# Loads and value products of the attention in another order, ahead of a fused expert network

## The chip, the cores and the metric

The kernel runs on one core of a Trainium2 chip. The metric is the device time of one launch in microseconds, as the median of several runs. One execution is also taken by the hardware profiler, and all rows below come from it.

## The reference

There are 12,480 tokens of 128 features (q, k, v, all float32) and 49 agents of 128 features. Three stages follow one another:

- Agent attention. The agents look at all keys: softmax over the 12,480 keys of scale * agents @ k.T, times v, gives 49 x 128 agent values. Every token then looks at the agents: softmax over 49 of scale * q @ agents.T, times the agent values. scale is 1 / sqrt(128).
- First expert layer: h = x @ w_in (128 to 2048), g = h where h > 0, else exp(h) - 1, then g @ w_out (2048 to 128).
- Second expert layer: h = y @ w_in2, g = max(h, 0) + alpha * min(h, 0) with one alpha per hidden feature, then g @ w_out2.

The result is 12,480 x 128 float32.

## The kernel before

**Three stretches.** A prologue computes the agents' attention over all keys. `normalize` turns its sums into agent values, and `fold` multiplies these with the first weight matrix, so that the main loop can go from a token's 49 shares straight to the first hidden layer. The main loop takes 25 blocks of 384 to 512 tokens and, in each, 8 units of 256 hidden features through four products: g1 (shares by folded weights), g2 (back to 128 features), g3 (second layer up), g4 (down). g3 and g4 run 10 units behind g1 and g2. Most products are split into a high and a low part, three matmuls for one.

**The prologue in pieces.** Keys and values are cut into ten pieces of 1280 tokens (the last of 960). For piece i, `scores` (S) makes 10 products with the agents (L478), copies them from PSUM with ACT (L488) and takes a running maximum with DVE (L491). Pieces 0 to 4 are one half, 5 to 9 the other. `max_down` (D) and `max_across` (X) turn a half's maximum into a row that every partition has (L500, L501, L502, L506). `weigh` (E) subtracts it with DVE (L511), exponentiates with ACT (L515) and sums on POOL (L518); the last piece of a half has DVE reduce the sum (L520). `values` (A) multiplies the weights with v's piece into one PSUM bank (L549); the fifth of each half copies the half's result out (L558). `shares` (N) makes the reciprocal of the sum (L529 to L540). Q are steps of the first token block's own softmax.

**The words.** The weights lie in memory as 64-bit words and are decoded on the chip. There are 16 slices, w0 to w15: w0 to w3 the first matrix, w4 to w7 the second, then wi2 (w8, w9, w10, w12) and wo2 (w11, w13, w14, w15). `decode` has three steps: two ACT instructions that read the words (L337, L338; this frees the word buffer), then DVE's two bit steps (L346, L349) and POOL's sum (L360, or L355 for w0 to w3), then ACT's high part and the low part (L366, L367), the latter on DVE for w8 and w9 and on POOL for the others. `micro(2)`, written T2 in the order, takes two such steps, from at most two slices in flight. What is left of the words when the prologue ends is decoded in the first slots of the main loop, two steps at each of four places of a slot from the second slot on; wo2 only after all four folds.

**What sets the order.** `LOADS` is the order in which SP issues the loads. `pump` goes down this list as far as buffers are free: k and v share a ring of nine, words have a ring of four. A k buffer is freed by its S, a v buffer by its A, and a word buffer by the first decode step. `ORDER` is the order in which the prologue's parts are written. S, D, X, E, A and N are written with a priority of 20. Only SP keeps the written order in the prologue (`PINNED`); the queues of PE, ACT, DVE and POOL are ordered at build time by a planner that looks at priorities, the written order and its own times for each instruction.

**PSUM.** The pairs of banks that S writes come from a ring of three, and a decode step of the prologue uses the same ring for its scratch (`spare`).

Of the kernel before, what the change touches and what calls it, by code (L numbers as in the profile page):

```python
# [36 lines left out]
SLICES += [("wi2", 0), ("wi2", 1), ("wi2", 2), ("wo2", 0), ("wi2", 3), ("wo2", 1), ("wo2", 2), ("wo2", 3)]  # L37
WO1, WI2, WO2 = [[SLICES.index((n, j)) for j in range(4)] for n in ("wo1", "wi2", "wo2")]
LOADS = """
    w0 k0 w1 k1 q0 w2 k2 w3 k3 w4 k4 k5 w5 k6 k7 k8 k9 w6 v0 v1 w7 v2 v3 v4 w8 v5 v6 w9 v7 v8 w10 v9 a0 q1  # L40
    w11 w12 w13 w14 w15
"""
ORDER = """
    T2 S0 T2 S1 Q2 T2 S2 Q2 S3 T2 Q2 S4 D0 Q2 T2 S5 X0 E0 Q2 S6 T2 E1 Q2 S7 E2 T2 S8 Q2 E3 T2 Q2 S9 D1 E4 A0 X1 A1 T2
    E5 A2 E6 T2 Q1 A3 E7 A4 E8 T2 A5 E9 N0 T2 A6 T2 A7 T2 A8 T2 A9
"""
PRIORITY = 20
REST_DVE = (8, 9)
# [771 lines left out]
```

## Time and profile before

| | |
|---|---|
| median of 3 runs | 1092.75 us (1092.57 to 1095.7) |
| profiled execution | 1091.42 us |
| its span, first to last instruction | 1089.3 us |
| PE busy | 1056.3 us (97%), mean granted clock 0.985 |
| DVE busy | 833.5 us (77%) |
| ACT busy | 818.2 us (75%) |
| POOL busy | 627.6 us (58%) |
| moved by DMA | 41.34 MB, mean 38 GB/s |

The slices of the page cut the span in 40 equal parts of 27.2 us; a digit is the busy share in tenths. A load of k or v is 640 KB (the last piece 480 KB), one of words 512 KB, of q for one block up to 256 KB. The score products and the value products appear as two PE instructions each, so a whole piece has 20.

### The profile page before, as it was taken

To read this page: it belongs to the slowest core of one execution; us is meant where nothing else is said; L and a number is where in the kernel's file an instruction comes from. 1 tells how busy PE (TensorE), PEld (TensorE's weight loads), DVE (VectorE), ACT (ScalarE), POOL (GpSimd) and SP (SyncE) were. 2 spreads that over 40 slices of the span, in tenths; PEclk is the share of its full clock that TensorE was granted. 3 is DMA by queue.
4 is the path that set the end of the run, shared out by engine and by line. 5 is a ranking of instruction groups with operands and counts; after the bars stand their busy time and mean duration, and the time that the engine had idled before them with its cause. 6 is when DMAs were issued, how large, how long until landed. Compare 5 with 4: busy or idle time off the path is not lost.

```text
span 1089.3 us, 13465 instructions
## 1 busy us (share of the span) xinstructions
PE 1056.3 (97%) x5045; PEld 839.5 (77%) x5045; DVE 833.5 (77%) x930; ACT 818.2 (75%) x954; POOL 627.6 (58%) x357
## 2 busy tenths in 40 slices
PE   7776999999999999999999999999999999999998
PEld 7744888888888877777777777777777777777776
DVE  5875588787878878878878788788788787888653
ACT  5687677778777787778777777877877777777763
POOL 3768555555655656556655665565565565565440
PEclk9878999999999999999999999999999999999999
DMA  9920000100100000010010010010010000000000
GB/s 359 371 86 19 10 18 19 28 10 20 29 19 19 20 20 19 20 29 11 21 29 11 21 29 10 20 30 10 20 30 13 27 20 18 23 10 20 10 1 20
DMA packets 17915, 41.34 MB, mean 38 GB/s; under 512 B 3345, under 2 KB 6303, under 8 KB 17851
## 3 DMA queue, kind: packets, MB, share of 16 engines
q1 hardware_dynamic: 17707, 40.36, 11.4%
q8 instruction: 40, 0.66, 0.3%
q14 instruction: 24, 0.20, 0.1%
q10 hardware_dynamic: 144, 0.13, 0.0%
HBM read 27.60 MB, written 6.39 MB: 31 GB/s over the span
## 4 chain that ended last, share of the span: by engine, by line
PE 90%; DVE 3%; POOL 2%; ACT 2%; issue 1%; DMA 1%; SPq 0%; POOLq 0%; DVEq 0%; ACTq 0%
PE o L418 10%; PE o L420 9%; PE o L419 9%; PE h L419 8%; PE h L420 8%; PE h L418 8%; PE h L617 8%; PE y L418 8%; PE y L419 8%; PE y L420 8%; PE h L620 4%; PE h L478 1%; POOL gl L646 1%; PE h L158 0%; PE h L157 0%
## 5 line engine op out<-in xcount | busy, mean ns | idle before, releaser
L646 POOL TENSOR_TENSOR gl<-g,gh 128x1024 fp32r<-128x1024 f32 (+2 forms) x200 | 468.4, 2347 | 264.4 <-DVE gh L637 169.9
L679 DVE SCALAR_TENSOR_TENSOR xl<-h,xh 128x1024 fp32r<-128x1024 f32 (+3 forms) x201 | 239.7, 1193 | 126.1 <-ACT xh L678 124.5
L678 ACT ACTIVATE xh<-h 128x1024 fp32r<-128x1024 f32 (+3 forms) x201 | 201.3, 1002 | 178.2 <-PE h L420 176.9
L635 DVE SCALAR_TENSOR_TENSOR g<-e,h 128x1024 f32<-128x1024 f32 (+2 forms) x200 | 236.5, 1183 | 80.7 <-ACT e L628 58.3
L627 ACT ACTIVATE e<-h 128x1024 f32<-128x1024 f32 (+2 forms) x200 | 199.3, 997 | 28.6 <-PE h L620 27.8
L628 ACT ACTIVATE e<-e 128x1024 f32<-128x1024 f32 (+2 forms) x200 | 208.1, 1040 | 6.1
L418 PE MATMUL o<-xh,wo2h 128*128 128x512 f32 (+2 forms) x400 | 161.8, 405 | 0.0
L419 PE MATMUL y<-gl,wo1h 128*128 128x512 f32 (+2 forms) x400 | 155.7, 389 | 2.4 <-POOL gl L646 2.4
L418 PE MATMUL h<-yh,wi2h 128*128 128x512 f32 (+2 forms) x400 | 154.3, 386 | 3.1 <-ACT yh L664 3.1
L418 PE MATMUL y<-gh,wo1h 128*128 128x512 f32 (+2 forms) x400 | 156.0, 390 | 0.0
L420 PE MATMUL y<-gh,wo1l 128*128 128x512 f32 (+2 forms) x400 | 154.9, 387 | 0.0
L420 PE MATMUL h<-yh,wi2l 128*128 128x512 f32 (+2 forms) x400 | 154.5, 386 | 0.0
L419 PE MATMUL h<-yl,wi2h 128*128 128x512 f32 (+2 forms) x400 | 154.5, 386 | 0.0
L420 PE MATMUL o<-xh,wo2l 128*128 128x512 f32 (+2 forms) x400 | 154.1, 385 | 0.0
L419 PE MATMUL o<-xl,wo2h 128*128 128x512 f32 (+2 forms) x400 | 153.8, 384 | 0.0
L617 PE MATMUL h<-pst,s 128*128 128x512 f32 (+2 forms) x400 | 110.1, 395 | 3.9 <-POOL gl L646 1.6
L637 DVE SCALAR_TENSOR_TENSOR gh<-e,h 128x1024 fp32r<-128x1024 f32 (+1 forms) x94 | 112.7, 1199 | 0.0
L644 ACT CAST gh<-g 128x1024 fp32r<-128x1024 f32 (+2 forms) x106 | 107.4, 1013 | 3.2 <-DVE g L635 3.1
L418 PEld LDWEIGHTS o<-xh,wo2h 128*128 128x128 f32 x400 | 74.9, 187 | 29.0 <-ACT xh L678 11.8
L617 PEld LDWEIGHTS h<-pst,s 128*128 128x128 f32 x400 | 75.5, 191 | 21.9 <-issue 2.6
L419 PEld LDWEIGHTS y<-gl,wo1h 128*128 128x128 f32 x400 | 76.0, 190 | 18.5 <-POOL gl L646 4.0
L418 PEld LDWEIGHTS h<-yh,wi2h 128*128 128x128 f32 x400 | 75.2, 188 | 17.8 <-ACT yh L664 3.4
(143 smaller groups left out, 1297.6 us busy)
## 6 DMA issues: line engine op xcount, KB each, us to landing
vt<-in_vm_dram SPq DMA_DIRECT2D x9, 640.0 KB
kt<-in_kT_dram SPq DMA_DIRECT2D x8, 640.0 KB
q<-in_qT_dram SPq DMA_DIRECT2D x18, 256.0 KB
psq<-pst SPq DMA_DIRECT2D x72, 64.0 KB
out_dram<-o SPq DMA_DIRECT2D x17, 256.0 KB
wi<-in_w_in_dram SPq DMA_DIRECT2D x8, 512.0 KB
wo<-in_w_out_dram SPq DMA_DIRECT2D x8, 512.0 KB
q<-in_qT_dram SPq DMA_DIRECT2D x6, 240.0 KB
```

The lines of the kernel that those rows point to most:

```text
L418: nc.tensor.matmul(out, w_hi, x_hi, start=start, stop=False)
L419: nc.tensor.matmul(out, w_hi, x_lo, start=False, stop=False)
L420: nc.tensor.matmul(out, w_lo, x_hi, start=False, stop=stop)
L617: nc.tensor.matmul(h_t[u + v][:, c, :], s1[:, i + 2 * v + c, :], pst[b][:, :n], start=True, stop=False)
L627: nc.scalar.activation(out=e, in_=h_t[u], func=AF.Relu, scale=-1.0)
L628: nc.scalar.activation(out=e, in_=e, func=AF.Exp, scale=-1.0)
L635: nc.vector.scalar_tensor_tensor(out=g, in0=e, scalar=-1.0, in1=h, op0=ALU.add, op1=ALU.max)
L637: nc.vector.scalar_tensor_tensor(out=gh, in0=e, scalar=-1.0, in1=h, op0=ALU.add, op1=ALU.max)
L644: nc.scalar.copy(out=gh, in_=g)
L646: nc.gpsimd.tensor_tensor(out=gl, in0=g, in1=gh.bitcast(F32), op=ALU.subtract)
L678: nc.scalar.activation(out=xh[:, c, :], in_=h[:, c, :], func=AF.Relu)
L679: nc.vector.scalar_tensor_tensor(out=xl[:, c, :], in0=h[:, c, :], scalar=0.0, in1=xh[:, c, :].bitcast(F32), op0=ALU.max, op1=ALU.subtract)
```

## The change

Two strings are changed and nothing else. In the loads, k2 comes ahead of w2, k4 ahead of w3, and so on; v0 to v9 start after k6 and lie between the last k; w5, w6 and w7 come between the later v, and w8, w9 and w10 after v9 and q1. In the order, A0 stands behind E1, A1 behind E2, A2 behind E3, A3 behind E4 and A4 behind X1, where all five stood behind E4 or later. Some T2 stand elsewhere, and there are thirteen of them instead of fifteen.

```diff
 LOADS = """
-    w0 k0 w1 k1 q0 w2 k2 w3 k3 w4 k4 k5 w5 k6 k7 k8 k9 w6 v0 v1 w7 v2 v3 v4 w8 v5 v6 w9 v7 v8 w10 v9 a0 q1
+    w0 k0 w1 k1 q0 k2 w2 k3 k4 w3 k5 k6 v0 w4 k7 v1 k8 v2 k9 v3 w5 v4 v5 w6 v6 v7 w7 v8 v9 a0 q1 w8 w9 w10
     w11 w12 w13 w14 w15
 """
 ORDER = """
-    T2 S0 T2 S1 Q2 T2 S2 Q2 S3 T2 Q2 S4 D0 Q2 T2 S5 X0 E0 Q2 S6 T2 E1 Q2 S7 E2 T2 S8 Q2 E3 T2 Q2 S9 D1 E4 A0 X1 A1 T2
-    E5 A2 E6 T2 Q1 A3 E7 A4 E8 T2 A5 E9 N0 T2 A6 T2 A7 T2 A8 T2 A9
+    T2 S0 T2 S1 Q2 T2 S2 Q2 S3 Q2 S4 D0 T2 Q2 S5 X0 E0 Q2 S6 E1 A0 Q2 T2 S7 E2 A1 T2 Q2 S8 E3 A2 T2 Q2 S9 D1 E4 A3 X1 T2 A4
+    E5 A5 E6 T2 Q1 E7 A6 E8 T2 E9 N0 T2 A7 T2 A8 T2 A9
 """
```

## Rows read from the trace of the kernel before

**Rows 1.** The page, PE's busy tenths in 40 slices of the span.
```profile
PE   7776999999999999999999999999999999999998
```

**Rows 2.** Windows of the start: busy us (x instructions) per engine, PEclk, DMA share, GB/s.
```profile
30.00:40.00 10.00, 8.97 (x112) 8.47 (x110) 9.35 (x18) 7.74 (x15) 9.10 (x8) 1.00 1.02 413
...
60.00:70.00 10.00, 7.56 (x34) 2.97 (x34) 8.47 (x15) 8.31 (x17) 5.68 (x5) 0.88 0.34 107
70.00:80.00 10.00, 8.98 (x34) 4.73 (x34) 8.76 (x15) 9.90 (x20) 9.52 (x7) 0.50 0.00 0
80.00:90.00 10.00, 6.67 (x28) 4.10 (x26) 7.50 (x8) 8.62 (x14) 9.83 (x9) 0.94 0.01 2
```

**Rows 3.** Timeline of PE: start, us, line, out<-in, count [idle before <-releaser].
```profile
6.09 8.93 PE L478 MATMUL h<-agd,kt 128*128 128x98 f32 x40 [6.09 <-ACT da L337]
...
25.64 0.44 PE L500 MATMUL o<-ident,pm 128*64 128x128 f32 x4 [0.67 <-DVE pm L493]
...
31.96 4.12 PE L478 MATMUL h<-agd,kt 128*128 128x98 f32 x36 [0.72 <-ACT S L488]
...
40.51 0.42 PE L506 MATMUL o<-ident,mb 49*128 49x49 f32 x2 [0.27 <-DVE mb L502]
40.86 2.39 PE L549 MATMUL y<-vt,S 128*49 128x128 f32 x40
...
49.01 5.82 PE L549 MATMUL y<-vt,S 128*49 128x128 f32 x60 [1.50 <-DVE avs L558]
...
54.76 1.28 PE L549 MATMUL y<-vt,S 128*49 128x128 f32 x20
57.57 0.54 PE L579 MATMUL o<-by,avs 128*128 128x160 f32 x2 [1.54 <-ACT by L540]
58.04 1.08 PE L549 MATMUL y<-vt,S 120*49 120x128 f32 x16
59.99 0.54 PE L579 MATMUL o<-by,avs 128*128 128x160 f32 x2 [0.87 <-DVE avs L558]
60.92 1.13 PE L590 MATMUL h<-w,avn 128*128 128x512 f32 x2 [0.38 <-DVE avn L580]
...
68.38 2.08 PE L590 MATMUL h<-w,avn 128*128 128x512 f32 x2 [0.58 <-DVE s1q L601]
```

**Rows 4.** Timeline of SP: issues of k3, w8 and the last v.
```profile
5.97 0.33 SPq L306 DMA_DIRECT2D kt<-in_kT_dram  x1
...
29.20 0.33 SPq L315 DMA_DIRECT2D wi<-in_w_in_dram  x1
...
39.65 0.41 SPq L311 DMA_DIRECT2D vt<-in_vl_dram  x1
```

**Rows 5.** Timeline of DVE, 40 to 53 us.
```profile
40.38 1.23 DVE L530 TENSOR_TENSOR mc<-mc 128x1 f32<-128x1 f32 x1
41.65 1.16 DVE L531 TENSOR_SCALAR cs<-mc 128x2 f32<-128x2 f32 x1
42.73 0.68 DVE L349 SCALAR_TENSOR_TENSOR dg<-da,h 128x512 uint32<-128x512 uint32 x1
43.32 2.85 DVE L511 TENSOR_TENSOR S<-S,o 128x490 f32<-128x490 f32 x5
...
51.77 0.87 DVE L367 TENSOR_TENSOR wi2l<-dg,wi2h 128x512 fp32r<-128x512 f32 x1 [2.09 <-ACT wi2h L366]
```

**Rows 6.** Timeline of POOL, 46 to 54 us.
```profile
46.99 1.27 POOL L367 TENSOR_TENSOR wo1l<-dg,wo1h 128x512 fp32r<-128x512 f32 x1 [0.61 <-ACT wo1h L366]
...
49.82 1.26 POOL L360 TENSOR_TENSOR dg<-dg,dr 128x512 uint32<-128x512 uint32 x1 [0.37 <-DVE dg L349]
51.04 2.48 POOL L518 TENSOR_TENSOR acc<-S,acc 128x490 f32<-128x490 f32 x2
```

**Rows 7.** Timeline of ACT, a word's high part and the next word's first step.
```profile
51.12 0.62 ACT L366 CAST wi2h<-dg 128x512 fp32r<-128x512 f32 x1 [2.50 <-POOL dg L360]
51.64 0.67 ACT L337 ACTIVATE da<-wi 128x512 f32<-128x512 f32 x1
```

## The prediction

> **What bounds the kernel now.** I began with the page's slices and took the windows for the first 100 us after them. From the fifth slice on (109 us) PE reads 9 in every slice but the last [rows 1]; the edits lie in the first 62 us, so all they can do is let that full stretch begin sooner or later. The windows split what comes before it [rows 2]. From 30 to 40 us DVE (9.35 of 10), POOL (9.10) and PE (8.97) are all nearly full. From 70 to 90 us POOL is full (9.52 and 9.83) while PE's clock is 0.50 and then 0.94.
>
> The timeline of PE gives the order of the attention [rows 3]. The scores run nearly without a break until 36.08 (S8 and S9: 36 instructions, 4.12 us, from 31.96). Two short waits interrupt them: 0.67 us before the first maxima (D0 at 25.64) and 0.72 us before S8. The value products A0 to A2 lie between there and X1, which ends at 40.93; A3 and A4 follow it (40 instructions in 2.39 us from 40.86, so 1.2 us each). Then PE has little to do: A5 to A7 start only at 49.01, A8 at 54.76, the first half of the normalization at 57.57, A9 behind it at 58.04, the second half at 59.99, the first fold at 60.92. So 24.8 us pass from the last score to the first fold.
>
> What fills them is not the loading. The timeline of SP shows this, once it is read as follows: each issue waits until the transfer eight issues earlier has landed [rows 4] (S0 starts 0.12 us after such a wait of its own piece, 6.09 against 5.97 [rows 3, 4]). By this k9 has landed at 29.20 and v4 at 39.65. Between them come w6 v0 v1 w7 v2 v3 v4, 5 x 640 + 2 x 512 = 4224 KB in 10.45 us: 404 KB per us. From v4 to v9 it is another 4576 KB, 11.3 us: v9 has landed near 51.0, and A9 uses it at 58.04, 7 us later. k9 lands before S8 starts. Neither transfer ends a wait on the chain.
>
> What fills them is DVE and POOL [rows 5, 6]. After X1, DVE spends 40.38 to 42.81 on two 128-element instructions of 1.2 us and then has a decode step, so that E5 starts at 43.32 and not at 40.93. On POOL the four sums of the second half stand between decode instructions: at 46.99 a word's remainder (1.27 us, after 0.61 of waiting), at 49.82 another word's sum (1.26, after 0.37), and only then the last two, done at 53.52. Normalization follows from there.
>
> **The change part by part.** I sum against the profiled execution's 1091.42 us (span 1089.3 and 2.1 around it); the median of the runs is 1.33 higher, and that is added at the end.
>
> *Loads.* Before v9 stand three words fewer (w8, w9, w10): 1536 KB at 404 per us, v9 3.8 us earlier, near 47.2. Before k9 stand three v more and one word fewer, 1408 KB: k9 3.5 us later, near 32.7. The order to come is S8 and then S9, and S9 is not reached before 34.2 (S8's share of 4.12 us after 31.96), so the later k9 is hidden by 1.5 us; if S9 came up without that cover, it would cost up to those 1.5 us. k2 to k6 land earlier by 512 or 1024 KB, 1.3 to 2.5 us, and earn nothing, since PE is busy with the scores before them. SP keeps its order, and each of v5 to v9 is queued behind the score or product that frees its buffer: v6 behind A0, which can't run before E0, near 30. SP has eight transfers in flight, some 4 MB or 10 us of work, so a wait of 2 or 3 us there starves nothing: cost 0, and it delays whatever SP has behind v6 by as much. Words w5, w6 and w7 land at about 35.5, 40 and 44.4 (1152 KB behind k9, and then 1792 each); w5 lay 2400 KB before k9, at 23.3, until now.
>
> *A0 to A2 between S6 and S9.* Three products of 1.2 us are 3.6 us, put into a stretch in which PE has 1.39 us of waits [rows 3]. If they fill both waits, S9 ends 2.2 us later; if none, 3.6; if the planner leaves them behind S9 as now, 0. Only SP keeps the written order, PE's is the planner's, which has put A9 behind the first half of the normalization, against the text. The row of S8's wait speaks for filling; I take +2.2. A3 and A4 fall into the waits for D1 and X1, where A0 to A2 are today: 0.
>
> *From S9 to the reciprocal.* The same instructions in the same order of dependence. At best DVE's 2.39 us and POOL's two decode instructions with their waits (1.27 + 0.61 + 1.26 + 0.37 = 3.5) go, some 5.5 us with what overlaps; at worst w6 and w7, now landing at 40 and 44.4, put two more instructions of 1.27 us between the sums, +2.5. Program order puts two decode steps fewer before E9, the later landing pushes the other way. I take 0.
>
> *A9.* If it precedes the first half of the normalization, the second half follows the first at 57.84 and not at 59.99: -2.15. If it stays behind: 0. Its nearest row is A8, which runs ahead (54.76). v9 lands 3.8 us sooner and its product no longer has a reason to come later than A8's does. I take -2.15.
>
> *Two T2 fewer.* Fifteen become thirteen. Counted step by step, the last decode step of the prologue was w10.1 and becomes w8.2: w8's third step, w9's second and third and w10's first move behind the fold, four steps. They are for POOL 1.27 us, for DVE 0.87 + 2 x 0.68 + 0.87 = 3.1, for ACT 0.62 + 0.62 + 2 x 0.67 = 2.6 [rows 5 to 7]. They land where POOL is full from 70 us on [rows 2]. If they fit in POOL's idle 4.3 us between 60 and 70 they cost 0; if DVE carries them in the chain, 3.1. POOL is the fuller of the two there, so I take its +1.27.
>
> Sum: 2.2 + 0 + 0 - 2.15 + 1.27 = +1.3, that is 1092.7 by the profile and **1094.0** as a median.
>
> *The clock.* From 70 to 80 us the granted clock is 0.50, the lower of the two levels, after PE's idle time of 43 to 57 us, and the fold pair takes 2.08 us there against 1.13 at 60.92 [rows 2, 3]. The Trainium skill ("TensorE: Matmul & The Clock Gate", Part 1: The HAM clock gate) says that the slow clock is the default and that activity releases it; by this, taking A0 to A2 away from 36 to 43 us is a cost of its own, because PE then does less between 43 and 57. The trace agrees in the order of events, and does not show whether the first two folds would be reached at the lower level.
>
> **The rivals.**
> *The chain shortens* (20%). The earlier v and the emptier DVE let the last sums run without decode between them. For it: POOL and DVE lose the work of w5 and w6 before 36 us. Against: those words then come at 40 to 48 us, just where the sums are. It takes 3.5 from POOL and 1.9 of DVE's 2.39: 1094.0 - 5.4 = 1088.6.
> *The words are late* (22%), the other side. Its place is POOL between 44 and 54 us: w7 lands at 44.4 and the chain needs POOL for four sums from about then, so two more decode instructions come between them (+2.5), and the four steps behind the fold cost DVE's 3.1 in place of 1.27 (+1.8): 1094.0 + 4.3 = 1098.3. It decides as soon as w7's decode stands ahead of the last sum on POOL. For it: POOL is in order and waited for such a step at 46.99 already.
> *PE reaches the folds at the lower clock* (8%). Folds 0 and 1 from 60.92 to 63.74 hold two pairs that take 0.95 more each there [rows 3], and their small products, by the same ratio, an estimated 0.2 more each: +2.3, 1096.3. Against it: A3 to A8 still lie before.
> *The planner undoes the move.* A0 to A2 stay behind S9 and A9 behind the normalization. Then only the four steps are left: 1091.42 + 1.27 + 1.33 = 1094.0, the forecast's own time by another way; it shares the forecast's chance.
>
> **How the numbers follow.** Forecast with the undone move 50%, its own range 1091 to 1096. 0.3% is 3.3 us, about what a measurement of this kernel can tell from no change, so the forecast counts as the same; the shortened chain as faster, 20%; late words and clock as slower, 30%. The range of 8 in 10 reaches to 1089 and to 1098.5: most of the shortened chain and most of the late words lie in it.
>
> **What would show it.** S9's last matmul at about 38.3 us shows the second term (36.1: the move was undone; 39.7: no wait was filled). A9 ahead of the first L579 shows the fourth. The first fold near 61 shows that the two cancel; at 57 or less the chain shortened, and the row to look at is the last sum on POOL (53.5 now). w8's remainder after the first fold, and POOL full until a microsecond later than now, show the last term. The forecast is wrong as a whole if the loading after all bounded the attention: then the first fold comes 3.8 us earlier, with no other row changed in length.

## The result and the profile after

The changed kernel takes **1104.65 us** (1103.33 to 1107.53, four runs), the one before 1092.66 beside it: ratio **1.0112 [1.0093, 1.0131]**, 12 us slower. The forecast was 1094.0, the range ended at 1098.5. The profiled execution spans 1103.4 us, 14.1 more than before.

The loss lies in the start. PE's slices are full again from the sixth, not the fifth [rows 1]. The chain that ended last has a new entry: DVE's L364, with 1% of the span after rounding. This line multiplies a wo2 word by 1 - alpha (`oma`), four times in all, and the four take 9.6 us together. The scores' L478 has 3%, where the same row of before has 1% and no L364.

The page after, PE's slices and the chain by line:

```profile
PE   7776799999999999999999999999999999999998
...
PE o L418 10%; PE o L420 8%; PE o L419 8%; PE h L617 8%; PE h L420 8%; PE h L419 8%; PE h L418 8%; PE y L418 8%; PE y L419 8%; PE y L420 8%; PE h L620 4%; PE h L478 3%; DVE dx L364 1%; POOL gl L646 1%; PE h L157 1%
```

A marker for the end of the start is the first of the 16 products that work alpha into the weights (L377), which has a fixed place in the loop. It moved from 117.1 to 130.3 us. First the row of before, then that of after:

```profile
L377 PE MATMUL h<-unit,wi2h x16: 219/274/276, 117.1 to 137.3; 128*128 128x128 f32 x16
```

```profile
L377 PE MATMUL h<-unit,wi2h x16: 219/274/277, 130.3 to 151.5; 128*128 128x128 f32 x16
```

PE's timeline after, to be read beside [rows 3]:

```profile
28.43 0.42 PE L506 MATMUL o<-ident,mb 49*128 49x49 f32 x2 [1.17 <-DVE mb L502]
28.78 4.10 PE L478 MATMUL h<-agd,kt 128*128 128x98 f32 x20
32.81 2.39 PE L549 MATMUL y<-vt,S 128*49 128x128 f32 x40
35.13 2.47 PE L478 MATMUL h<-agd,kt 128*128 128x98 f32 x20
37.53 1.30 PE L549 MATMUL y<-vt,S 128*49 128x128 f32 x20
38.76 1.92 PE L478 MATMUL h<-agd,kt 128*120 128x98 f32 x16
...
57.95 2.15 PE L549 MATMUL y<-vt,S 128*49 128x128 f32 x36
62.96 1.70 PE L579 MATMUL o<-by,avs 128*128 128x160 f32 x4 [2.86 <-ACT by L540]
65.04 2.08 PE L590 MATMUL h<-w,avn 128*128 128x512 f32 x2 [0.38 <-DVE avn L580]
...
95.21 0.69 PE L419 MATMUL y<-gl,wo1h 128*128 128x384 f32 x1 [4.09 <-POOL gl L646]
...
116.32 1.94 PE L617 MATMUL h<-pst,s 128*128 128x480 f32 x4 [2.40 <-DMA pst<-pst]
```

S9 ends at 40.68 (36.08 before) and the first fold starts at 65.04 (60.92): 4.1 us. Another 9 us go after that. The windows show where: PE has 3.40 of 10 between 90 and 100 us, and DVE has 9.11 with only seven instructions in it. Before that POOL has 3.69 and 6.33 from 60 to 80 us, where it had 5.68 and 9.52 [rows 2]: its decode comes later.

```profile
60.00:70.00 10.00, 6.65 (x26) 2.21 (x24) 6.99 (x13) 4.54 (x11) 3.69 (x3) 0.66 0.50 158
70.00:80.00 10.00, 6.21 (x29) 2.54 (x22) 8.21 (x14) 9.21 (x17) 6.33 (x5) 0.67 0.19 54
80.00:90.00 10.00, 9.75 (x38) 5.79 (x36) 8.82 (x15) 9.95 (x19) 10.00 (x8) 0.64 0.00 0
90.00:100.00 10.00, 3.40 (x11) 2.33 (x11) 9.11 (x7) 6.14 (x10) 8.23 (x7) 0.70 0.00 0
```

DVE's timeline after, and POOL's beside it:

```profile
88.33 1.82 DVE L635 SCALAR_TENSOR_TENSOR g<-e,h 128x768 f32<-128x768 f32 x2
90.99 6.49 DVE L364 TENSOR_TENSOR dx<-w,oma 128x512 f32<-128x512 f32 x1 [0.84 <-POOL w L360]
97.41 0.63 DVE L215 TENSOR_REDUCE s<-d 32x15 f32<-32x480 f32 x1
98.49 0.69 DVE L364 TENSOR_TENSOR dx<-w,oma 128x512 f32<-128x512 f32 x1
```

```profile
89.67 2.50 POOL L360 TENSOR_TENSOR w<-w,dr 128x512 uint32<-128x512 uint32 x2
92.13 1.27 POOL L367 TENSOR_TENSOR wo2l<-dx,wo2h 128x512 fp32r<-128x512 f32 x1
93.35 3.58 POOL L646 TENSOR_TENSOR gl<-g,gh 128x768 fp32r<-128x768 f32 x2
98.62 0.68 POOL L232 TENSOR_SCALAR s<-s 32x15 f32<-32x15 f32 x1 [1.69 <-DVE s L223]
```

One instruction that takes 0.69 us at 98.49 takes 6.49 at 90.99. It ends 0.55 us after POOL's unbroken stretch, which ends at 96.93. Behind it on DVE stands L215, the sums of block 1's softmax (97.41; 81.72 before), whose input ACT has finished at 91.43. Then comes the DMA that spreads the shares, and at 116.32 block 1's first g1 still waits 2.40 us for that DMA's data. In before the longest L364 took 1.90 us.

The last words are issued late too. SP's timeline, before and then after; the last of the issues is done at 62.56 and at 73.31:

```profile
55.79 6.77 SPq L315 DMA_DIRECT2D wo<-in_w_out_dram  x3
```

```profile
59.41 0.33 SPq L315 DMA_DIRECT2D wi<-in_w_in_dram  x1
60.54 12.77 SPq L315 DMA_DIRECT2D wo<-in_w_out_dram  x3
```

In all, the issues of words (L315) wait 4.8 us before and 18.6 us after for ACT to read a word and so free its buffer. SP's waits, before and then after (us in total, times, longest):

```profile
SPq L315 <- ACT dr L338: 4.8, 2, 2.8
```

```profile
SPq L315 <- ACT dr L338: 18.6, 4, 7.5
```

### The profile page after: what moved, and what is told of

Read it like the earlier page. It is cut to its first block, busy times and chain, and to the rows that moved or that the text cites. A ratio compares the mean times of both kernels' runs of the same rounds, so it can differ in the third digit from the quotient of the medians.

```text
span 1103.4 us, 13469 instructions
## 1 busy us (share of the span) xinstructions
PE 1063.7 (96%) x5045; PEld 843.7 (76%) x5045; DVE 837.6 (76%) x930; ACT 818.0 (74%) x954; POOL 628.2 (57%) x357
## 3 DMA queue, kind: packets, MB, share of 16 engines
HBM read 27.60 MB, written 6.39 MB: 31 GB/s over the span
## 4 chain that ended last, share of the span: by engine, by line
PE 92%; DVE 3%; POOL 2%; ACT 1%; DMA 1%; issue 1%; SPq 0%; POOLq 0%; ACTq 0%; DVEq 0%
PE o L418 10%; PE o L420 8%; PE o L419 8%; PE h L617 8%; PE h L420 8%; PE h L419 8%; PE h L418 8%; PE y L418 8%; PE y L419 8%; PE y L420 8%; PE h L620 4%; PE h L478 3%; DVE dx L364 1%; POOL gl L646 1%; PE h L157 1%
## 5 line engine op out<-in xcount | busy, mean ns | idle before, releaser
L635 DVE SCALAR_TENSOR_TENSOR g<-e,h 128x1024 f32<-128x1024 f32 (+2 forms) x200 | 236.3, 1183 | 81.5 <-ACT e L628 63.6
L418 PEld LDWEIGHTS y<-gh,wo1h 128*128 128x128 f32 x400 | 76.3, 191 | 15.4 <-ACT gh L644 1.0
```

Of the source, the lines that this page charges most:

```text
L418: nc.tensor.matmul(out, w_hi, x_hi, start=start, stop=False)
L635: nc.vector.scalar_tensor_tensor(out=g, in0=e, scalar=-1.0, in1=h, op0=ALU.add, op1=ALU.max)
```

## The experiments

Ratios are to the kernel before on the same chip, with 95% intervals. "Marker" is the first L377 product.

**The two strings apart.** e1 has the new `LOADS` with the old `ORDER`; e2 the reverse. e3 and e4 keep the new `ORDER` and change the new loads: e3 puts k7 to k9 ahead of v0 to v2, e4 puts the words back among the pieces.

```diff
 e3 LOADS
-    w0 k0 w1 k1 q0 k2 w2 k3 k4 w3 k5 k6 v0 w4 k7 v1 k8 v2 k9 v3 w5 ...
+    w0 k0 w1 k1 q0 k2 w2 k3 k4 w3 k5 k6 k7 w4 k8 k9 v0 v1 v2 v3 w5 ...
 e4 LOADS
+    w0 k0 w1 k1 q0 w2 k2 w3 k3 w4 k4 k5 w5 k6 v0 k7 v1 k8 v2 k9 w6 v3 w7 v4 w8 v5 v6 w9 v7 v8 w10 v9 a0 q1
```

> The new order of the loads with the old order of the parts (fifteen T2). Theory one, late words: w5 to w7 land some 12 us later, so the decode moves behind the fold whatever the parts' order is; nearly the whole loss is here, 1100 to 1106 us, with POOL's last decode instruction after 95 us. Theory two, products between the scores: the planner has A0 to A3 before S9 here too, so S9 ends at 39 to 41 us, but the decode has its two T2 back: 1096 to 1099 us.

> The new order of the parts (thirteen T2) with the old loads. Theory one, late words: the words are early, only four decode steps move: 1093 to 1097 us. Theory two, products between the scores: the planner leaves A0 to A4 behind S9 here, so nothing of the loss: 1090 to 1095 us with S9 done near 36 us. If the two missing T2 are the cause, 1100 us or more.

> The changed kernel with k7, k8 and k9 loaded ahead of v0, v1 and v2; the words stay as late as in the change. Theory two, products between the scores: S9 ends 2 to 4 us earlier than in the change and the first fold too: 1099 to 1102 us. Theory one, late words: the decode behind the fold is as in the change, within 1.5 us of it: 1103 to 1106 us.

> The changed kernel with the words at their old places among the loads, k and v mixed as in the change. Theory one, late words: most of the loss goes, 1093 to 1097 us. Theory two, products between the scores: A0 to A2 still run before S9, so the loss stays above half: 1099 us or more.

| | ratio | S9 ends | first fold | last word issued | marker | longest L364 |
|---|---|---|---|---|---|---|
| before | 1 | 36.08 | 60.92 | 62.56 | 117.1 | 1.90 |
| after | 1.0112 [1.0093, 1.0131] | 40.68 | 65.04 | 73.31 | 130.3 | 6.49 |
| e1 loads only | 1.006 [1.0042, 1.0079] | 39.05 | 63.75 | 61.91 | 126.0 | 5.30 |
| e2 order only | 1.0035 [1.0021, 1.005] | 35.30 | 57.85 | 63.86 | 123.1 | 6.39 |
| e3 k first | 1.0036 [1.0021, 1.0051] | 36.15 | 62.30 | 67.23 | 124.4 | 6.24 |
| e4 words as before | 1.0067 [1.0043, 1.0091] | 39.27 | 61.52 | 66.23 | 126.2 | 6.25 |

By the medians e1 (1099.96), e2 (1097.42) and e3 (1097.47) lie in no theory's range; e4 (1101.23) lies in that of theory two. e1 shows that the loads alone cost 6.6 us (by the ratio), e2 that the order alone, with its thirteen T2, costs 3.8.

The loads set PE's order, not the written order. e1, with `ORDER` as before, has four value products ahead of S9. e2, with the new `ORDER`, has none: its timeline of PE runs S7 and S8, S9, and only then A0 and A1.

```profile
28.45 4.71 PE L478 MATMUL h<-agd,kt 128*128 128x98 f32 x40
33.38 1.92 PE L478 MATMUL h<-agd,kt 128*120 128x98 f32 x16 [0.23 <-DVE top L491]
35.23 2.39 PE L549 MATMUL y<-vt,S 128*49 128x128 f32 x40
```

e2 folds 3.1 us earlier than before and is still slower. So a theory by the fold's time fails, and all four kernels share a long L364. In e2 the two L364 from 81.67 (6.39 and 0.68 us) stand beside POOL's stretch that ends at 87.52, and POOL then waits for what they feed. e2's DVE, then its POOL:

```profile
81.67 7.00 DVE L364 TENSOR_TENSOR dx<-w,oma 128x512 f32<-128x512 f32 x2
```

```profile
83.94 3.58 POOL L646 TENSOR_TENSOR gl<-g,gh 128x768 fp32r<-128x768 f32 x2
88.80 1.27 POOL L367 TENSOR_TENSOR wo2l<-dx,wo2h 128x512 fp32r<-128x512 f32 x1 [1.28 <-ACT wo2h L366]
```

**Without the instruction.** e5 is the changed kernel, e6 the one before, without the four multiplications by 1 - alpha.

```diff
-        if name == "wo2":
-            v = dec.tile([P, 4, P], U32, tag="dg", bufs=2, name="dx").bitcast(F32)
-            nc.vector.tensor_tensor(out=v, in0=gf, in1=oma[:, sl].unsqueeze(2).to_broadcast([P, 4, P]), op=ALU.mult)
-            gf = v
```

> The changed kernel without the multiplication of wo2 by 1 - alpha (L364, four DVE instructions; that part of the computation is left out). Theory: the loss behind the fold is one DVE instruction of two SBUF inputs that gets no turn while POOL works without a pause (6.49 us in the changed kernel, 5.3 to 7.0 in the four variants, at most 1.9 before): 1097 to 1100 us, that is 5 to 7 less than the change. Rival, late decode work on POOL: POOL's work is the same, so 1102 to 1105 us.

> The kernel before without the same four instructions (that part of the computation is left out). Theory: it pays at most 2 us for them, so 1090 to 1093 us. Rival, that DVE's load as such sets the start: 5 us less here too, 1087 to 1089 us.

e5: 1.004 [1.0023, 1.0057], 6.5 us less than the changed kernel by the medians (1104.65 to 1098.15) and 7.9 by the ratios. e6: 1.0 [0.9985, 1.0016]. The four instructions are worth nothing that can be measured in the kernel before, and 6.5 us or more in the changed one, though e5's fold (65.98) and last word (74.57) are as late as the changed kernel's. The 7.0 us in e5's expectation is e2's row of two instructions; the longest single one there is 6.39.

**Another engine, another form.** The multiplication goes to ACT, or stays on DVE with one tensor as its input.

```diff
-            nc.vector.tensor_tensor(out=v, in0=gf, in1=oma[:, sl].unsqueeze(2).to_broadcast([P, 4, P]), op=ALU.mult)
 e7, e9, e10, e11, e12, e14
+            for f in range(4):
+                nc.scalar.activation(out=v[:, f, :], in_=gf[:, f, :], func=AF.Copy, scale=oma[:, 4 * j + f:4 * j + f + 1])
 e8
+            for f in range(4):
+                nc.vector.tensor_scalar(out=v[:, f, :], in0=gf[:, f, :], scalar1=oma[:, 4 * j + f:4 * j + f + 1], scalar2=None, op0=ALU.mult)
```

> The new order of the parts with the old loads, and the multiplication by 1 - alpha on ACT, four instructions of 128 columns for each word, in place of DVE. Theory: it keeps its fold at 58 us, 3 us ahead of the kernel before, and loses the 5 us that DVE waited: 1089 to 1093 us. If ACT, 9.9 of 10 full from 70 to 80 us, is now the bound: 1095 to 1098 us.

> The same with the multiplication left on DVE, as four tensor_scalar instructions with one SBUF tensor each and the factor per partition. If only instructions with two SBUF tensors are held up by POOL, none of them is long and the time is 1090 to 1094 us. If every DVE instruction from SBUF to SBUF is held up (a small one, L538, took 0.93 us), the first of the four takes 4 us or more and the time is 1096 to 1099 us.

> The whole changed kernel with the multiplication by 1 - alpha on ACT. Theory: the held-up DVE instruction is some 6 of the change's 12 us and the later scores and fold are the rest: 1097 to 1100 us, first fold still near 65. Rival, the late words are what remains of it and ACT is too full for the extra work: 1102 us or more.

> The changed kernel with k7 to k9 ahead of v0 to v2 and the multiplication on ACT: both suspected costs taken away, the words as late as in the change. Theory: 1090 to 1093 us, no more than the kernel before. If the late words cost something of their own: 1095 us or more.

> The kernel before with the multiplication on ACT. It tells whether the 5 us of the new order with ACT come from the order. Theory: the kernel before has no held-up instruction, so 1091 to 1095 us. If ACT's instructions are the gain: 1088 us as with the new order.

| | base | ratio | first fold | last word issued | marker |
|---|---|---|---|---|---|
| e7 | e2, on ACT | **0.995 [0.9934, 0.9966]** | 57.02 | 63.02 | 113.7 |
| e8 | e2, one tensor on DVE | 1.004 [1.0024, 1.0055] | 56.92 | 62.92 | 121.2 |
| e9 | after, on ACT | 1.0075 [1.0045, 1.0105] | 65.97 | 74.57 | 130.7 |
| e10 | e3, on ACT | 0.9978 [0.9962, 0.9994] | 60.12 | 65.05 | 116.6 |
| e11 | before, on ACT | 0.9997 [0.9981, 1.0013] | 59.92 | 61.57 | 117.0 |

e7 beats both kernels: 1088.02 us against 1093.51, 1 us below the range expected of it. ACT does each 128 columns in 0.40 us, none longer than 0.41, with POOL at 8.65 of 10 between 70 and 80 us:

```profile
L365 ACT ACTIVATE dx<-w,oma x16: 388/396/411, 67.7 to 85.9; 128x128 f32<-128x128 f32 x16
```

In e8 the instruction of one tensor is held up as well, 3.48 us for one of 0.28; the fold is as early as e7's, the marker 7.5 us later, the time 1097.63 us. Its group (min/median/max in ns), and one set of four:

```profile
L365 DVE TENSOR_SCALAR dx<-w,oma x16: 270/284/3479, 65.8 to 89.3; 128x128 f32<-128x128 f32 x16
```

```profile
76.83 5.00 DVE L365 TENSOR_SCALAR dx<-w,oma 128x128 f32<-128x128 f32 x4
```

So ACT's gain is not its spare time but that it isn't held. e11 shows that it is worth nothing where nothing is held up. e10 came as expected (1091.68); but its last word is issued at 65.05, so it does not tell what words as late as the change's cost. e9 missed: 1097 to 1100 was expected, 1102.63 came, where its rival had put it. So a second cause was open, with two suspects: the late words, and an ACT too full for the extra work (9.90 and 9.97 of 10 from 80 to 100 us in e9).

**The two T2.** Two T2 are put back, one between S3 and S4 and one between S6 and E1: in e7 (e12), in the changed kernel (e13), and in e9 (e14).

```diff
-    T2 S0 T2 S1 Q2 T2 S2 Q2 S3 Q2 S4 D0 T2 Q2 S5 X0 E0 Q2 S6 E1 A0 Q2 T2 ...
+    T2 S0 T2 S1 Q2 T2 S2 Q2 S3 T2 Q2 S4 D0 T2 Q2 S5 X0 E0 Q2 S6 T2 E1 A0 Q2 T2 ...
```

> The new order of the parts with the old loads and the multiplication on ACT, and the two missing T2 put back (fifteen). If the earlier fold (57 us) comes from the two decode steps less in the prologue, the fold is at 59 to 61 us and the time 1090 to 1094; if it comes from the parts' places, fold at 57 and 1086 to 1089 us.

> The changed kernel with its two missing T2 at the places of before (between S3 and S4, and behind S6). If the words' late decode is what is left of the loss, the last word is loaded near 62 to 65 us and not at 73, and the time is 1098 to 1101 us. If the later scores are all of it, 1103 to 1106 us.

> The same with the multiplication on ACT. If late decode and the held-up instruction are both costs of the change, 1094 to 1097 us; if the later scores are the rest, 1099 to 1103 us.

| | ratio | first fold | last word issued | marker | longest L364 |
|---|---|---|---|---|---|
| e12 | 0.9963 [0.9947, 0.9979] | 58.96 | 60.60 | 117.4 | on ACT |
| e13 | 1.0031 [1.0016, 1.0045] | 65.99 | 65.81 | 124.8 | 2.23 |
| e14 | 1.0032 [1.0018, 1.0046] | 64.18 | 64.01 | 121.7 | on ACT |

With old loads the thirteen T2 cost nothing (e7 against e12, 1.4 us the other way, less than the intervals), though the fold is 1.9 us later with fifteen. With the new loads they cost 4.7 us (e9 against e14), and with the multiplication on DVE 8.8 (after against e13). e13 folds 1 us later than the changed kernel and is 8.8 us faster, more than was expected of it (1096.85 us); e14 (1096.08) came as expected. In e13 the last word is issued 7.5 us earlier than in the changed kernel, and its longest L364 is short:

```profile
89.06 2.23 DVE L364 TENSOR_TENSOR dx<-w,oma 128x512 f32<-128x512 f32 x1
```

## Why the prediction was wrong

**Two steps failed, "Two T2 fewer" and "Loads".** "Two T2 fewer" stood in the sum at 1.27 us with 3.1 as the upper end; the runs have 8.8 in its place (e13 against the changed kernel). "Loads" stood at 0; the runs have 6.6 for the loads alone (e1) and 7.5 under the new order (e14 against e12). The first counted the four steps' instructions at their usual durations and asked where they fit. It missed two things.

*The words.* I counted steps and forgot that the first step of a word frees a buffer, and so releases a load. With the new loads and two T2 fewer, the last issue waits until ACT has read w11, and is done at 73.31 (65.81 in e13, where the waits for ACT's reading are 12.6 us and not 18.6). ACT's row, after:

```profile
72.28 0.67 ACT L338 ACTIVATE dr<-wo 128x512 uint32<-128x512 uint32 x1
```

With the multiplication on ACT the two T2 cost 4.7 us, 3.6 us either way (e9, e14). e4 points the same way: thirteen T2 with earlier words issue the last one at 66.23 and gain 4.9 us, with an L364 as long as ever. But its fold is 3.5 us earlier too, so it does not set the words apart. "The words are late" had named the right kind of cause, at the wrong place (POOL between 44 and 54 us) and price (1098.3). On POOL the words did not come between the sums: from X1's end to the last sum it was 8.8 us, 12.6 before.

*The duration of an instruction is not its own.* [Rows 5] gave DVE's two-input instructions 0.87 us. Beside a POOL without a pause one L364 takes 6.49. I had seen POOL at 9.52 and 9.83 [rows 2] and took it for the fuller engine, not for one that could stop DVE. [Rows 5] held a sign of it: I took the 1.2 us of the two 128-element instructions for their own length, but L531, 1.16 there beside one of POOL's sums, takes 0.23 in the changed kernel, where POOL has no work beside it:

```profile
47.95 0.23 DVE L531 TENSOR_SCALAR cs<-mc 128x2 f32<-128x2 f32 x1
```

Putting the multiplication on ACT gains 4.0 us in the changed kernel (after against e9), hardly more than the two intervals together (3.9). It gains 6.3 with k first (e3 against e10) and 9.3 with the old loads (e2 against e7), so it is not a constant.

The Trainium skill ("SBUF — State Buffer", Who interferes with whom) says that a DVE instruction with two SBUF inputs contends with a GpSimd instruction that reads SBUF, and that the one second to issue is blocked until the first is through. The traces agree on who is held: L364 and e8's form are, while L635, which reads PSUM, takes 0.91 each from 88.33 with POOL busy all along. They differ in how long: when L364 is free to start, at 90.99, POOL is in the first of four instructions of 1.2 to 1.8 us without a pause between them, and L364 waits not for one of them but for all four (the L364 at 86.49 waited for one, as the last section shows).

**A0 to A2** stood at +2.2 for S9's end; it is +4.6. The three products are 3.6 of it. S7 lost as well, which the term did not have: S6 was done before D0 and did not fill the wait for X0, PE waited 1.17 for `mb`, and S7 then took 4.10 where S8 took 2.47, at a granted clock of 0.77 and then 0.50 (28 to 32 us). The two come to more than 4.6; waits that are gone pay the rest, the 0.72 ahead of S8 [rows 3] among them.

**From S9 to the reciprocal and A9** stood at 0 and -2.15. A9 does precede the first half of the normalization, as said (57.95 against 62.96), and from `by` to the fold it is 2.56 us in place of 3.83. The parts between are off in both directions: +2.0 from S9 to X1, -3.8 from X1 to the last sum on POOL, +2.6 from there to `by`. With these the fold is 4.1 us late, where the sum had it near 61.

**"Loads" asked only whether PE would wait for a transfer**, and called the later k9 hidden by 1.5 us. PE doesn't wait for k9 in the changed kernel, and yet the loads cost 6.6 us or 7.5. They do so in part by the order that the planner makes of them: A0 to A3 come ahead of S9 without a word of `ORDER` changed (e1), and S9 ends at 39.67 in e14 and at 35.64 in e12. e3, which only lets k7 to k9 pass v0 to v2, ends S9 at 36.15 and takes back 8.3 us; its last word is issued 6.1 us earlier as well, so how much of that is S9's is not shown. In e1 the fold is 2.8 us late, and the other 3.8 stand beside an L364 of 5.30. Earlier v earned nothing, as forecast of the loading.

**The lower clock** did come at the first fold (2.08 us a pair at 65.04), as the rival had it. It is not the main cause: e10 has it at the first fold too (2.07) and is no slower than the kernel before (0.9978), and e7 has 0.50 from 70 to 90 us and is faster. What share it has in the changed kernel no run shows.

**The account**, by ratios times 1093, each about 2 to 4 us either way: `ORDER` with its thirteen T2, on ACT, -5.5 (e7); the new loads under it +13.7 (e7 to e9); the multiplication on DVE instead of ACT +4.0 (e9 to after); together +12.2. Another path splits it otherwise: e12 -4.0, loads +7.5, two T2 fewer +4.7, DVE +4.0. The two T2 fewer cost something only under the new loads, while the loads cost 7.5 us with all fifteen T2 in place.

**What stays open.** The marker orders the kernels only roughly: e12's is 0.3 us later than before's and e12 is 4.0 us faster, so some of the gain lies behind it. e5's words are as late as e9's and e5 is 3.8 us faster (3.8 either way). e5 leaves the multiplication out, where e9 gives ACT sixteen instructions of 0.40 us while ACT is full; so what late words cost depends on the work behind them, and no run takes the words and the full ACT apart. Of e14's 3.5 us I can't say how much is the later fold, since no run has k first and the T2 back.

## What to carry to other kernels

Before a decode step is moved, ask which buffer it frees and which load waits for that buffer: four steps priced at 1.3 us cost 4.7 under the new loads, with the hold on DVE taken out. Before loads are moved, ask what order the planner will make of them, and not only whether an engine waits for one. Where DVE and POOL both work out of SBUF and POOL has no pause, let the price of a two-input DVE instruction range from its own 0.7 us to the rest of POOL's unbroken stretch, or give it to ACT. And a milestone on the way (the first fold) is no forecast of the end: e2 folded 3.1 us earlier and was slower, e13 1 us later than the changed kernel and 8.8 us faster.

## What was not expected of the hardware

DVE can be kept waiting through several POOL instructions that follow one another without a pause. L364 (0.69 us at its shortest in the changed kernel) took 5.30 to 6.49 us in five kernels; in the changed one it ended 0.55 us after the last of POOL's stretch.

It is not always so. The L364 before that one (86.49) ended 0.55 us after the one POOL instruction that was running, and the next on POOL, an L367, took 1.73 us where the one at 92.13 took 1.27. DVE, then POOL, after:

```profile
86.49 1.12 DVE L364 TENSOR_TENSOR dx<-w,oma 128x512 f32<-128x512 f32 x1
```

```profile
85.24 1.82 POOL L646 TENSOR_TENSOR gl<-g,gh 128x768 fp32r<-128x768 f32 x1
87.03 1.73 POOL L367 TENSOR_TENSOR wi2l<-dg,wi2h 128x512 fp32r<-128x512 f32 x1
```

In the kernel before POOL has no pause from 70.48 to 84.16 either, and the two L364 that start in that stretch took 0.75 and 1.90 us. So a POOL without a pause is not enough for a long hold, and what decides who goes next no run here shows.

A `tensor_scalar` of 128x128 in float32, with one tensor read from SBUF, was held to 3.48 us against a median of 0.284, so two tensors are not needed. Small ones suffer too: L502 on 49x128 took 1.27 us while POOL ran a remainder (0.48 in the kernel before). The cost comes back on POOL, which at 98.62 had itself waited 1.69 us for what DVE could not finish.

```profile
45.54 1.27 DVE L502 COPY mb<-mc 49x128 f32<-49x128 f32 x1
```
